# New instruction orders for two spectral convolutions and the attention front between them, and a strided read of kernel rows

## The chip, the cores and the metric

The kernel runs on one core of a Trainium2 chip. The metric is device time in microseconds (us) of one execution; lower is better. Five engines work in parallel and each takes its instructions in the order of the program: PE (matrix products into PSUM), VectorE (DVE), ScalarE (ACT), GpSimd (POOL) and SyncE (SP), which issues most DMA transfers.

## The reference, cut to what matters

Four layers follow each other on an activation `x` of 2048 rows and 512 columns in bf16, each with a layer normalisation ahead of it and a residual addition behind:

```python
x = x + _A_ref(_layernorm(x), A_wqkv, A_wo)      # sliding-window attention, 32 heads, 8 keys at distances 0, 2, .. 14
x = x + _B_ref(_layernorm(x), B_A_re, ..., B_Dskip)   # long convolution
x = x + _A_ref(_layernorm(x), A_wqkv, A_wo)
x = x + _B_ref(_layernorm(x), B_A_re, ..., B_Dskip)

def _B_ref(u, A_re, A_im, B_re, B_im, C_re, C_im, log_dt, Dskip):
    ...
    logdA, dB = dt * A, dt * Bc
    l = jnp.arange(L).astype(A_re.dtype)           # bf16: positions above 256 are rounded
    K = jnp.einsum("dn,dnl,dn->dl", Cc, jnp.exp(logdA[:, :, None] * l), dB).real
    ...                                             # y = causal convolution of u with K, by FFT of length 2 L
    return y + u * Dskip[None, None, :]
```

Both convolutions use the same filter `K` (one row of 2048 per column). Because the positions are in bf16, those from 256 on fall on even numbers, from 512 on multiples of four, and so on: `K` has only 641 different rows of 512 values.

## The kernel before

The program has stages, one after the other in each engine's stream:

1. *Filter and first front*: `k_gen` computes the 641 rows into a DRAM tensor `kd`, and beside it the first normalisation, queries and keys.
2. *First attention core*: `LayerA.core` with the order string `CORE0`. On the way `k_half_load` calls `k_load` twice (half the columns each): it fills `kr`, 128 partitions of 16 positions, from `kd`, with transfers issued by SyncE. `k_half_fix` (line 1501) adds `Dskip`; `k_part` (line 1505) reorders `kr` into `k_perm`.
3. *First convolution*: `FftB.run` with `ORDER0`.
4. *Rest of the first convolution and second front*: `FftB.run` with `ORDERF`.
5. *Second attention core* with `CORE1`; it begins with the last pieces of the front.
6. *Second convolution* with `ORDER1`, which ends in the stores to the output.

No scheduler chooses the order within a stage: each string is a list of tokens, worked off from left to right, and each token emits its instructions. What happens when is then set by the engines' in-order streams, by semaphores and by buffers. A convolution splits the columns into two groups g of 64 x 4, and has these tokens:

- `K`, `U` (`f1`, line 822): 16 matrix products transform a piece of the filter or of the input; 8 pieces for each group.
- `k`, `u` (`f2`, line 829): the second step, 16 small matrix products, 8 pieces for each group. `k` leaves the spectrum in a buffer; SyncE then issues two transfers that copy it with its halves swapped (line 854) and GpSimd issues one that keeps it in DRAM for the second convolution (line 855). `u` is always cast by ScalarE into one of three buffers `ub` (line 880).
- `m` (`u_mult`, line 868): VectorE multiplies `ub` by the spectrum and its swapped copy. In the second convolution the spectra come from DRAM through a ring (lines 858 and 860), ten pieces ahead.
- `y`, `Y` (`i1`, lines 894 and 898): back-transform, 8 pieces for each group; all eight `m` of the group must be done.
- `w`, `v`, `z` (lines 924 to 948): last step and residual addition into `x_sb`, for 8, 4 and 4 rows; the digits are group, half of its columns (not for `z`) and block of rows.

The letter behind a token names the engine that takes the result out of PSUM: `A` is ScalarE, `D` VectorE. With `D` a `w`, `v` or `z` piece is added by VectorE; with `A` PE adds the residual with further products and ScalarE casts. The PSUM tiles of a convolution (line 811 for the casts) come from two pools of two, taken round: a piece can be written once the piece four before it has been taken out.

Small letters at the start of `ORDER0` finish the first attention's last rows and their normalisation: `s`, `t` statistics, `g` aggregation, `r` reciprocal root on ScalarE, `a`, `e` the offsets, `c0` to `c7` the application (on GpSimd without a letter), `q` masks on GpSimd.

In `ORDERF` the convolution's last pieces stand between the front's: `h` and `H` statistics of half or whole rows (block b of four rows), `a` aggregation (line 1554), `p` reciprocal root (ScalarE, lines 155 and 156), `n` application (line 197; `G` shares it between GpSimd and VectorE), `T` transposes on PE (line 271), `E` their casts (line 273), `P` key projections (line 282, cast in line 285), `Q` query projection (line 223), `x` the shifted copy of keys (line 295), `S` the change of PSUM pools. `CORE1` begins with the pieces `P30`, `P31`, `x0`, `x2`, `P32`, `Q01`, `e0`, `Q02` and then the first product of queries and keys (line 342).

Of the kernel before, what the change touches and what calls it, by code (L numbers as in the profile page):

```python
# [21 lines left out]
S = 2048  # L22
# [27 lines left out]
lxzzppzEzektKxxkkkKEKteepkkkkKKkkkUUkUUUUUUEKKUoUUUUkkkoKkoUUpxxqqKQppxXXXpZZxxZ  # L50
"""
ORDER0 = """
KD a q KA c3 c1 t s KA KA KD KA g r KD e c2 KA KD KA c6 c0 c5A KD c7 kA kD c4D KA kA kD KA KD UA KD
UA UA UD KA UD UA UD UA kA kD kA kD u UD u UA UA m UD u u m m u u UA m m u u kD UA UA m m UA kD kA
kD m u u u kD kD kA kA m m m yA u u YA yD m yA m u u u yA YA yA m m m w000D yD yA YD yA YA yD yA
w010D
"""
ORDERF = """
yA h00 YA h01 v100A v110D h10 a0 z12A p0 z11A n0D h11 w001A w011A S a1 p1 T0 E01A z13A E00D n1G H2
P02 a2 P00 Q00 p2 T1 E10D E11D P01 P11 P12 n2D H3 a3 P13 T2 P10 E20D E21D P03 p3 P21 P22 n3D P23 T3  # L60
E30D E31A P20 x1
"""
ORDER1 = """
UA UD UA UD UA UA UD UA UD UD u u m m u u m m UA u UA UD m UA u u UD UA u m m u u m m u YD m u YA YA
m u yD m yA u u m m u w001A m m yA yA w000D YA yD yA YD w011D yA yD w010D yA yD yA v101A v103D v113A
v102D v112D v111D v110A v100A
"""

CORE0 = """
# [927 lines left out]
def bf16_round_np(x):  # L997
    x = np.ascontiguousarray(np.asarray(x, dtype=np.float32)); u = x.view(np.uint32)
    return ((u + 0x7FFF + ((u >> 16) & 1)) & 0xFFFF0000).view(np.float32)
# [409 lines left out]
def k_load(tc, nc, kr, kd, ds_):  # L1409
    l = np.arange(2048, dtype=np.float32)  # L1410
    m = bf16_round_np(l).astype(np.int64).reshape(128, 16) - 16 * np.arange(128)[:, None]
    nc.sync.dma_start(kr[0:16], kd[0:256, ds_].rearrange("(p a) d -> p a d", a=16))
    n = 1
    for o, (p0, p1, base) in enumerate(((16, 32, 256), (32, 64, 384), (64, 128, 512))):
        s = 2 << o
        blk = m[p0:p1]
        assert (blk == blk[0:1]).all() and (blk % s == 0).all()
        row = [int(v) for v in blk[0]]
        np_ = p1 - p0
        q = 16 // s  # L1420
        runs = []
        for v in range(0, 17, s):
            c = [a for a in range(16) if row[a] == v]
            assert c == list(range(c[0], c[-1] + 1))
            runs.append((v // s, c[0], len(c)))
        for (t, a0, cnt) in runs:
            rows = kd[base + t:base + t + (np_ - 1) * q + 1:q, ds_]
            nc.sync.dma_start(kr[p0:p1, a0:a0 + cnt, :],
                                                              rows.unsqueeze(1).to_broadcast([np_, cnt, D // 2]))
            n += 1  # L1430


@with_exitstack
def kernel(
# [58 lines left out]
    def k_half_load(h):  # L1493
        hs = slice(h * 256, (h + 1) * 256)
        kr = krp.tile([P, NA, D // 2], BF16, name=f"k_rl{h}")
        k_load(tc, nc, kr, kd, hs)
        krs[h] = kr
# [136 lines left out]
```

## Time and profile before

| | us |
|---|---|
| three runs | 396.95, 397.65, 400.25; median 397.65 |
| profiled execution: time | 397.01 |
| profiled execution: span on the core | 395.2 |
| busy: PE, DVE, ACT, POOL | 349.7, 377.4, 333.0, 43.2 |
| granted PE clock, mean | 0.996 |

The span is the time from the first to the last instruction on the core; the execution's own time has 1.8 us more around it. Stage bounds in the profiled execution: first cast of the first convolution at 183.78, last product of it at 230.40, first key projection of the second front at 247.47, first product of the second core at 263.18, first cast of the last convolution at 350.58. In a timeline row the columns are start, length, engine, line, operation, output and inputs, count, and in brackets the idle time before it with what ended it; `SPq` is SyncE's DMA queue. In a row of a waits view they are who waited for whom, the total, the count and the longest.

### The profile page before, as it was taken

Reading aid. Unit: us, or ns where it says so; the run is one execution under the profiler, and the core shown is the slowest. Engines: PE = TensorE matmul, PEld = TensorE weight load, DVE = VectorE, ACT = ScalarE, POOL = GpSimd, SP = SyncE. Lnnn points to the kernel's source line nnn. Section 1 sums busy time; section 2 is a strip of 40 time slices with the busy share of each in tenths; the row PEclk is TensorE's granted clock in tenths of the full one; section 3 lists DMA queues with packets and bytes.
Section 4 is the critical chain, followed back from the end, with each engine's and each line's share of the span. In section 5 each row is a group of like instructions: output and inputs, shape, how many; then the busy total and the mean of one; then the engine's idle time right before and its main releaser. Section 6 shows DMA issues by size and latency. Waiting matters only on the chain.

```text
span 395.2 us, 15021 instructions
## 1 busy us (share of the span) xinstructions
PE 349.7 (88%) x6598; PEld 240.5 (61%) x6598; DVE 377.4 (95%) x453; ACT 333.0 (84%) x594; POOL 43.2 (11%) x93
## 2 busy tenths in 40 slices
PE   3967568899999999999997889999999998887896
PEld 2225336585645677666886878543456676566885
DVE  6999999999999999999999999979999999989995
ACT  7999999999568789989999987675566899989974
POOL 9400100000370001002422200100000001000000
PEclk9999999899999999999999999999999999999999
DMA  7952811214125746494463844820153029504507
GB/s 211 398 162 35 86 53 25 71 29 87 57 50 133 211 149 195 111 347 172 174 237 131 309 124 109 307 67 0 40 162 95 3 78 347 157 14 152 174 3 215
DMA packets 63695, 54.18 MB, mean 137 GB/s; under 512 B 33033, under 2 KB 49966, under 8 KB 63374
## 3 DMA queue, kind: packets, MB, share of 16 engines
q1 hardware_dynamic: 61958, 48.70, 41.6%
q0 software_dynamic: 1664, 4.52, 3.1%
q8 instruction: 51, 0.84, 0.9%
q14 instruction: 14, 0.11, 0.1%
q10 hardware_dynamic: 8, 0.00, 0.0%
HBM read 30.15 MB, written 13.24 MB: 110 GB/s over the span
## 4 chain that ended last, share of the span: by engine, by line
DVE 35%; PE 32%; ACT 14%; issue 8%; DMA 7%; SPq 2%; POOL 1%; DVEq 0%; ACTq 0%; POOLq 0%
DVE pav L467 9%; PE pq L398 7%; ACT a1s L811 4%; PE pk L1323 4%; PE pp L1261 4%; PE pp L282 3%; PE pq L223 3%; DVE A_t L1157 3%; DVE prod L342 3%; DVE B_t L1157 3%; DVE t L868 2%; DMA w_sb<-w_dram 2%; PE L L350 2%; ACT ub L880 2%; DVE x_sb L946 2%
## 5 line engine op out<-in xcount | busy, mean ns | idle before, releaser
L467 DVE TENSOR_TENSOR pav<-attn,v_ext 128x4096 bf16<-128x4096 bf16 (+1 forms) x34 | 72.0, 2160 | 0.3
L342 DVE TENSOR_TENSOR prod<-qT,kT_ext 128x4096 bf16<-128x4096 bf16 x29 | 65.2, 2285 | 0.7 <-PE L L350 0.5
L1157 DVE TENSOR_TENSOR A_t<-A_t,pow_t 128x1024 bf16<-128x1024 bf16 (+4 forms) x46 | 38.0, 871 | 0.4
L492 PEld LDWEIGHTS <-pav 64*128 64x128 bf16 x1664 | 26.4, 95 | 14.1 <-DVE pav L467 6.7
L880 ACT CAST ub<-pb 128x1024 bf16<-128x1024 f32 x32 | 31.9, 1091 | 1.6 <-PE pb L829 1.0
L492 PE MATMUL po<-ident,pav 64*128 64x64 bf16 x1664 | 29.1, 191 | 4.6 <-ACT oT L484 1.8
L509 PE MATMUL pq<-wop,oT 128*128 128x512 bf16 x128 | 32.8, 380 | 0.3 <-ACT oT L494 0.2
L829 PE MATMUL pb<-a1s,w_sb 128*128 128x64 bf16 x768 | 27.6, 193 | 5.1 <-ACT ub L880 1.8
L398 PE MATMUL pq<-wv,xnT 128*128 128x512 bf16 x128 | 30.5, 380 | 0.0
L1261 PE MATMUL pp<-xnT,kT_ext 128*128 128x512 bf16 x96 | 24.7, 390 | 5.8 <-ACT xnT L1254 3.3
L829 PEld LDWEIGHTS <-w_sb 128*128 128x128 bf16 x768 | 24.9, 98 | 7.6 <-issue 5.9
L811 ACT CAST a1s<-pb 128x1024 bf16<-128x1024 f32 x29 | 28.1, 1064 | 1.1 <-PE pb L822 1.1
L400 ACT CAST v_ext<-pq 128x512 bf16<-128x512 f32 x32 | 18.6, 586 | 12.0 <-PE pq L398 11.9
L225 ACT CAST qT<-pq 128x512 bf16<-128x512 f32 x24 | 14.0, 584 | 12.8 <-PE pq L223 12.8
L1323 PEld LDWEIGHTS <-A_t 128*64 128x64 bf16 (+1 forms) x512 | 22.0, 105 | 4.5 <-issue 1.4
L1323 PE MATMUL pk<-B_t,A_t 128*64 128x84 bf16 (+1 forms) x512 | 23.9, 204 | 0.6 <-ACT kgs L1331 0.6
L811 DVE CAST a1s<-pb 128x1024 bf16<-128x1024 f32 x19 | 22.5, 1216 | 1.4 <-PE pb L822 1.3
L223 PE MATMUL pq<-xnT,kT_ext 128*128 128x512 bf16 x96 | 23.7, 380 | 0.0
L398 PEld LDWEIGHTS <-xnT 128*128 128x128 bf16 x128 | 11.7, 98 | 13.6 <-issue 1.3
L509 PEld LDWEIGHTS <-oT 128*128 128x128 bf16 x128 | 11.5, 98 | 12.7 <-ACT oT L494 2.2
L822 PE MATMUL pb<-F1c,xnT 128*64 128x128 bf16 x256 | 17.3, 219 | 1.6 <-ACT a1s L811 0.6
L1261 PEld LDWEIGHTS <-kT_ext 128*128 128x128 bf16 x96 | 8.7, 98 | 16.3 <-issue 8.4
(281 smaller groups left out, 911.9 us busy)
## 6 DMA issues: line engine op xcount, KB each, us to landing
w_sb<-w_dram SPq DMA_DIRECT2D x32, 256.0 KB, 5.7
w_dram<-xnT SPq DMA_DIRECT2D x1, 4096.0 KB
kf_ring<-kf_dram SPq DMA_DIRECT2D x13, 256.0 KB, 3.9
kf_ring<-kf_dram SPq DMA_DIRECT2D x26, 128.0 KB, 3.9
v_ext<-v_ext SPq DMA_DIRECT2D x4, 784.0 KB, 6.2
x_blk<-in_A_x_dram SPq DMA_DIRECT2D x4, 512.0 KB, 4.9
kT_ext<-in_A_wqkv_dram SPq DMA_DIRECT2D x4, 512.0 KB, 9.5
x_sb<-in_A_x_dram SPq DMA_DIRECT2D x4, 512.0 KB, 7.4
```

What stands on the lines that cost most here:

```text
L223: nc.tensor.matmul(pq[:], lhsT=self.wqk[:, dt, ft * P:(ft + 1) * P], rhs=self.xnT[:, dt, q * 512:(q + 1) * 512], start=(dt == 0), stop=(dt ...
L342: nc.vector.tensor_tensor(pr, self.qT[q][:, ft].unsqueeze(1).to_broadcast([P, W, 4, P]), kap, ALU.mult)
L398: nc.tensor.matmul(pp[:], lhsT=xnT[:, dt, a * P:(a + 1) * P], rhs=wv[:, dt, :], start=(dt == 0), stop=(dt == NDT - 1))
L467: nc.vector.tensor_tensor(pv[:, i], attn[:, n % 4].unsqueeze(2).to_broadcast([P, W, DH // parts, H]), vap, ALU.mult)
L492: nc.tensor.matmul(po[:, h, 0, i * nt + ft, :], lhsT=pvf[rows, i, w, ft * P:(ft + 1) * P], rhs=ident[rows, rows], start=(w == 0 and ft + i ...
L509: nc.tensor.matmul(pw[:], lhsT=oT[:, ftp, :], rhs=self.wo[:, ftp, :], start=False, stop=(ftp == NDT - 1), skip_group_check=ahead)
L811: (self.nc.scalar.copy if eng == "act" else self.nc.vector.tensor_copy)(dst, src)
L829: nc.tensor.matmul(p2[:, j, :], lhsT=self.w2[:, ec * EC + j, :], rhs=a1s[:, ec * EC + j, :], start=True, stop=True)
L880: nc.scalar.copy(ub[:], p2)
L1157: return lambda: nc.vector.tensor_tensor(*args)
L1261: nc.tensor.matmul(pps[kind, b, ft][:], lhsT=la.wqk[:, dt, c:c + P], rhs=la.xnT[:, dt, b * 512:(b + 1) * 512], start=(dt == 0), stop=(dt = ...
L1323: nc.tensor.matmul(o, lhsT=lhs, rhs=Bt[:, ri, c * CH + ql].rearrange("p b g -> p (b g)"), start=(not half and j % 4 == 0 and ri == 0), sto ...
```

## The change

Three order strings are replaced: `ORDER0`, `ORDERF` and `ORDER1`; `CORE0`, `CORE1` and `ORDERK` stay. The tokens are the same but for these: in `ORDER0` one `UD` becomes `UA`; in `ORDERF` `v100A` becomes `v100D` and `E20D` becomes `E20A`; in `ORDER1` one `yA` becomes `YA`, `v110A` becomes `v110D`, and `w011D` is split into `v012D` and `v013A`.

In `k_load` the second region (partitions 16 to 32, positions 256 to 511) has nine runs of equal positions, of 2, 1, 3, 1, 3, 1, 3, 1 and 1 places. It was read by nine transfers, one for each run, each row repeated as often as the run is long. Now four transfers read it: transfer c fills the places c, c + 4, c + 8 and c + 12 of every partition from every second row of `kd`. The bytes are the same. The two other regions take at most eight runs and keep their transfers. `k_load` runs twice, so ten transfers go. (The counter `n`, which nothing reads, goes too.)

```diff
 ORDER0 = """
-KD a q KA c3 c1 t s KA KA KD KA g r KD e c2 KA KD KA c6 c0 c5A KD c7 kA kD c4D KA kA kD KA KD UA KD
-UA UA UD KA UD UA UD UA kA kD kA kD u UD u UA UA m UD u u m m u u UA m m u u kD UA UA m m UA kD kA
-kD m u u u kD kD kA kA m m m yA u u YA yD m yA m u u u yA YA yA m m m w000D yD yA YD yA YA yD yA
-w010D
+q a KD KA t c2 KA KA s c1 g KD r c0 e KA KD c3 c5A KA KD KA KD c6 c4D KA c7 kA kD KA KD UA UA KD UA
+UD KA UD UA UD UA kA kD kA kD kA kD u u kD m UA UA UA UD UA m u kD u u m m kA UA kD kD u u UA UA m u
+m m kD u m kA u kA m u m u u m m yA YA yD m u u u m m m yA yA YA yD w000D yA yA YD yA YA yD yA w010D
 """
 ORDERF = """
-yA h00 YA h01 v100A v110D h10 a0 z12A p0 z11A n0D h11 w001A w011A S a1 p1 T0 E01A z13A E00D n1G H2
-P02 a2 P00 Q00 p2 T1 E10D E11D P01 P11 P12 n2D H3 a3 P13 T2 P10 E20D E21D P03 p3 P21 P22 n3D P23 T3
-E30D E31A P20 x1
+h00 yA YA v100D v110D w011A h10 a0 h01 p0 z11A n0D z12A h11 S w001A T0 a1 E01A p1 z13A E00D n1G P03
+H2 Q00 P00 T1 a2 p2 P01 P02 E10D E11D n2D H3 a3 P11 P12 T2 E20A P10 E21D p3 n3D P13 P21 x1 P20 T3
+E31A E30D P22 P23
 """
 ORDER1 = """
-UA UD UA UD UA UA UD UA UD UD u u m m u u m m UA u UA UD m UA u u UD UA u m m u u m m u YD m u YA YA
-m u yD m yA u u m m u w001A m m yA yA w000D YA yD yA YD w011D yA yD w010D yA yD yA v101A v103D v113A
-v102D v112D v111D v110A v100A
+UA UD UA UD UA UA UD UA UD UD u u m UA m u UA UD UA m u UD m u u UA m m u u u m u m m m u u YD YA YA
+m u yD yA m m yA u u w000D YA YA m m u m w001A v013A v012D w010D yD yA YD yA yD yA yD yA v102D v101A
+v111D v112D v110D v100A v103D v113A
 """
...
 def k_load(tc, nc, kr, kd, ds_):
...
-    n = 1
     for o, (p0, p1, base) in enumerate(((16, 32, 256), (32, 64, 384), (64, 128, 512))):
...
+        if len(runs) > 2 * s:
+            for c in range(2 * s):
+                t = row[c] // s
+                assert row[c::2 * s] == [row[c] + 2 * s * i for i in range(q // 2)]
+                rows = kd[base + t:base + t + np_ * q, ds_].rearrange("(p i) d -> p i d", i=q)[:, 0::2]
+                nc.sync.dma_start(kr[p0:p1, c::2 * s, :], rows)
+            continue
         for (t, a0, cnt) in runs:
             rows = kd[base + t:base + t + (np_ - 1) * q + 1:q, ds_]
             nc.sync.dma_start(kr[p0:p1, a0:a0 + cnt, :],
                                                               rows.unsqueeze(1).to_broadcast([np_, cnt, D // 2]))
-            n += 1
```

## The prediction

> **What bounds the kernel now.** I read the page first (whole span), then busy time in stretches cut where the orders meet, then VectorE's own waits, then the timelines of VectorE, ScalarE and SyncE inside each stretch. Lengths are us.
>
> ```profile
> span 395.2 us, 15021 instructions
> core 0: us, PE busy (x) PEld busy (x) DVE busy (x) ACT busy (x) POOL busy (x), PEclk, DMA share, GB/s
> 183.78:203.21 19.43, 18.25 (x556) 16.56 (x552) 19.15 (x25) 19.20 (x23) 8.91 (x14) 1.00 0.42 151
> 203.21:230.40 27.19, 22.14 (x685) 19.99 (x680) 26.25 (x24) 26.59 (x30) 4.63 (x9) 1.00 0.68 238
> 230.40:247.47 17.07, 16.23 (x346) 14.66 (x347) 15.53 (x40) 12.50 (x18) 0.64 (x1) 1.00 0.35 96
> 247.47:263.18 15.71, 15.71 (x108) 8.49 (x108) 13.67 (x36) 10.61 (x21) 1.04 (x2) 1.00 0.68 236
> 263.18:350.58 87.40, 82.99 (x1577) 48.93 (x1577) 85.47 (x72) 66.41 (x143) 1.03 (x1) 1.00 0.33 101
> 350.58:379.83 29.25, 24.93 (x727) 23.13 (x721) 28.63 (x25) 28.26 (x31) 0.00 (x0) 1.00 0.35 111
> 379.83:395.20 15.37, 11.37 (x352) 10.84 (x352) 10.67 (x12) 7.69 (x10) 0.00 (x0) 1.00 0.47 139
> ```
>
> The rows are: first convolution up to its last product (two rows), its tail with the start of the second front, the rest of that front, the second attention core, the last convolution, its tail. In the first two, VectorE (45.40 of 46.62) and ScalarE (45.79) are both full. In the third and fourth PE is the full one (31.94 of 32.78). In the core, and in the last convolution until its tail, VectorE is full. So a new order can only win the small gaps that are left; it can lose freely.
>
> ```profile
> DVE ln_nb L185 <- ACT ln_rstd L156: 1.4, 2, 0.8
> DVE t L868 <- DMA kn<-kn: 0.9, 1, 0.9
> DVE z L811 <- PE pb L898: 0.6, 1, 0.6
> DVE xnT L273 <- PE pt L271: 0.5, 1, 0.5
> DVE kT_ext L295 <- ACT kT_ext L285: 0.4, 1, 0.4
> ```
>
> These are VectorE's longest waits between 183 and 264 (total, times, longest). Only the second lies in the first convolution: a product waits for the transfer that swaps one kernel spectrum's halves.
>
> **The kernel rows.** Ten of SyncE's transfers go (five per half); the bytes stay, and so do the runs of 256 elements.
>
> ```profile
> 155.52 10.02 SPq L1428 DMA_DIRECT2D k_rl<-kd_dram  x17
> 165.65 10.99 SPq L599 DMA_DIRECT2D w_sb<-w_dram  x16
> 176.95 0.43 DVE L1505 COPY k_perm<-k_rl 128x1024 bf16<-128x1024 bf16 x1 [0.23 <-DMA w_sb<-w_dram]
> L829 PE MATMUL pb<-a1s,w_sb x512: 188/193/204, 189.4 to 224.7; 128*128 128x64 bf16 x171
> ```
>
> Seventeen issues took 10.02, 0.59 each, so five fewer free SyncE's queue about 2.9 earlier, in each half. The reader of the second half comes at 176.95, some 11 after the last of those issues; its 0.23 stands before an instruction with eight semaphores to look at. The cover is VectorE's attention products. Behind the reads in the queue stand the table stores and w_sb loads, whose first reader is the spectrum transform at 189.4. I take 0; ends -0.23 (the wait goes) and +0.6 (a strided transfer costs one more issue). Without the cover it would be worth 2.9.
>
> **First convolution, to its last product.** Each token of the order is a PE piece into one of four PSUM buffers, taken round, and a cast by VectorE or ScalarE; `m` is a VectorE product. `UD` fell from 5 to 4 and `UA` rose from 11 to 12; all else is permutation.
>
> ```profile
> 228.13 2.35 DVE L868 TENSOR_TENSOR t<-ub,kf_nat 128x2048 bf16<-128x2048 bf16 x2
> 193.27 6.53 ACT L811 CAST a1s<-pb 128x1024 bf16<-128x1024 f32 x7
> 225.78 1.22 DVE L868 TENSOR_TENSOR t<-ub,kn 128x2048 bf16<-128x2048 bf16 x1 [0.94 <-DMA kn<-kn]
> 227.09 1.01 ACT L880 CAST ub<-pb 128x1024 bf16<-128x1024 f32 x1 [0.59 <-DVE t L868]
> ```
>
> A VectorE piece takes 1.13 (2.35 - 1.22), a ScalarE cast about 0.92. VectorE ends the last product at 230.40 (the 228.13 row, 2 pieces, next piece at once). It loses one cast (1.13) and may lose the 0.94: floor 230.40 - 2.07 = 228.3. On ScalarE 46 casts stand up to the last `ub` in both orders (one `UA` more, one `yA` fewer ahead of it), so the last `ub` comes at 228.1 less its own 0.59 wait: 227.5, and the last product ends no earlier than 228.7. Laying the new sequence out by hand with these two durations and four buffers, I find VectorE waits of 0.55 at `UD11` (three `UA` in a row stand before it) and some 0.1 at each of four later products, and the last product at 229.0.
>
> The swaps and their queue then decide.
>
> ```profile
> 200.74 1.10 SPq L854 DMA_DIRECT2D kf_sb<-kf_sb  x2
> 206.70 2.07 SPq L854 DMA_DIRECT2D kf_nat<-kf_nat  x1
> 214.66 1.10 SPq L854 DMA_DIRECT2D w_sb<-w_sb  x2
> 224.01 2.81 SPq L854 DMA_DIRECT2D kf_nat<-kf_nat  x4
> kn<-kn SPq DMA_DIRECT2D x12, 128.0 KB, 4.7
> w_sb<-w_sb SPq DMA_DIRECT2D x4, 128.0 KB, 2.9
> ```
>
> Before, four spectra were swapped early, then four in a burst (8 transfers, 200.74 to 208.77: 1.00 each), one later, and seven in the last run (14 transfers, 214.66 to 226.82: 0.87 each, landing after 4.7). The new order moves two of the early ones (k2, k3) behind all U transforms, so seven (k2 to k8) come in one run, then four, then three: 28 transfers nearly without a gap, from 199.8 (one ScalarE cast before the old 200.74). By 0.87 the last is issued at 223.6 and lands at 228.3; the last product is due at 227.9. So it waits 0.4 and ends at 229.4, against 230.4. By 1.00 it lands at 231.9: that is the slow rival. I take 0.87, from the longer run of the two: **-1.0**; ends -1.7 and +2.6. Spreading the last three is what removes the old 0.94.
>
> **Its tail and the second front.**
>
> ```profile
> 235.93 1.22 DVE L946 TENSOR_TENSOR x_sb<-pb,x_sb 128x1024 bf16<-128x1024 f32 x1 [0.23 <-PE pb L944]
> 237.19 2.71 DVE L150 BATCH_NORM_STATS2 ln_bn<-x_sb 128x6 f32<-128x256 bf16 x8
> 239.82 0.67 DVE L946 TENSOR_TENSOR x_sb<-pb,x_sb 128x512 bf16<-128x512 f32 x1
> 246.43 0.99 ACT L273 COPY xnT<-pt 128x1024 bf16<-128x1024 bf16 x1
> 247.47 0.81 PE L282 MATMUL pp<-xnT,kT_ext 128*128 128x512 bf16 x3 [0.23 <-ACT xnT L273]
> 263.18 2.29 DVE L342 TENSOR_TENSOR prod<-qT,kT_ext 128x4096 bf16<-128x4096 bf16 x1
> ```
>
> One y more stands after the last `ub` on ScalarE (+0.92), which cancels part of the lead for the first piece of group 1; `w000D`, no longer behind the last product and a y, gives its buffer back sooner. I keep -0.8 at `w010D` (235.93). In the front, `v100` goes to VectorE (0.67) and `E20` to ScalarE (about 1.0), PE loses four small matmuls; `h01` moves behind `a0` and covers the wait for `p0` (0.5 of the 1.4), but half its old cover of `v100` goes (0.4). `E01A` moves ahead of `p1`, so PE no longer waits for it at 247.47; `E00D` ends 1.0 earlier. From there to the first product PE has the same 15.71 of work, and the order puts small waits in: `P21` on `E20A`, `E21D` (0.2), `x2` on `P23` (0.3). At 263.18 I keep **-0.6**. Bounds: -2.5 if PE's 0.84 of gaps goes too, +2.6 with the slow swaps. `p3` stands behind one more ScalarE piece; if `n3` slips, `T3` and all of the core slip with it.
>
> **The core** (263.18 to 350.58) keeps its order and its waits: 0.
>
> **Last convolution.**
>
> ```profile
> 386.73 1.21 DVE L811 CAST z<-pb 128x1024 bf16<-128x1024 f32 x1
> 388.18 0.69 DVE L946 TENSOR_TENSOR x_sb<-pb,x_sb 128x512 bf16<-128x512 f32 x1 [0.24 <-PE pb L944]
> 390.87 1.25 ACT L948 CAST x_sb<-pb 128x512 bf16<-128x512 f32 x2 [1.43 <-PE pb L944]
> 384.61 7.91 SPq L1597 DMA_DIRECT2D out_dram<-x_sb  x8
> ```
>
> VectorE loses `w011D` (1.13) and gains `v012D` and `v110D` (0.6 each): level. ScalarE changes `v110A` for `v013A`: level. The g0 additions move ahead of the g1 y pieces, and the last two additions go to two engines at once, not both to ScalarE (1.25): -0.6 there, less 0.2 for `m15`, whose `ub` now stands behind two whole `YA`. The eight small additions are still PE's, and the last store still takes 395.2 - 392.1 = 3.1. **-0.4**; ends -0.8 and +0.7 (the last three products, with `w000D` ahead of them, wait for two casts).
>
> **The sum.** 0 - 0.6 - 0.4 = -1.0. The profiled execution took 397.0 (span 395.2 and 1.8 around it), so 396.0. The median of the runs shown, 397.65, lies 0.65 above it: 396.6.
>
> **The rivals.**
> *Slow swaps (slower).* Place: SyncE's queue from 199.8, with the kf_dram stores on the same DMA engines. Price: at 1.00 per transfer the last product ends at 233.0, 2.6 late; all behind it is 2.6 late, less 0.4 at the end: 397.65 + 2.2 = 399.9. It decides from about 0.91 per transfer (28 x 0.04 = 1.1 eats the lead); the burst's six kf_nat transfers alone went at 1.14 (201.95 to 208.77), and at that the price would be 6.0. For it: 0.68 DMA share in 203.21:230.40 and the 2.07 issue in the burst; against: the old last run kept 0.87.
> The Trainium skill, "DMA: Bandwidth & Descriptors", section "Latency and other measured facts", has HBM answering in 0.2 us on average and 2 us at high load, the largest part of a transfer's fixed cost. The landing rows agree in kind (2.9 for w_sb, 4.7 for kn). If the longer run loads HBM more than the old one, as an estimate from that page up to 1.8 us would come on the last landing, and the forecast would become 398.4; this is why I give the slow side more than the fast.
> *No change.* PE is full in 230.40:263.18, and the extra y and the waits in the front take back the 1.0; the end gains nothing as PE's additions set it: 397.6. For it: 15.71 of 15.71; against: PE waits that the old order shows at 247.47.
> *All gaps go.* 228.7 for the last product, PE without its 0.84, -0.8 at the end: -1.7 - 0.8 - 0.8 = -3.3, 394.3. For it: VectorE idles 4.8 from 183.78 to 263.18; against: every wait removed there stands before a full PE.
> *It doesn't do what it says:* the four reads could leave the queue as slow as nine; it costs nothing (first part), so this is inside "no change".
>
> **How the numbers follow.** Forecast (about 395.5 to 397.2) 0.44, slow swaps 0.26, no change 0.20, all gaps 0.10. The predicted time is 396.6. The range takes in both rivals' ends: 394.0 to 400.6. One per cent, about what a measurement of this kernel can tell from no change, is 4.0. Beyond -4.0 goes only the last case, if PE's busy time, whose ends are modelled, hides more gaps than it shows: 0.09. Beyond +4.0 goes the slow rival from 1.08 per transfer on: 0.17. Within: 0.74.
>
> **What would show it.** Right: no product in the first convolution waits over 0.6 for a DMA; last product at 229 to 230; first product of the second core near 262.6; the last two additions start within 0.7 of each other on two engines; k_rl issues take 7 per half with no reader nearer. Wrong: `t<-ub` waits for swaps of 1 or more from the ninth on; PE gaps behind `T2` or `T3`; VectorE idle between 351 and 388; a wait at a k_perm copy.

## The result and the profile after

| | kernel before | changed kernel |
|---|---|---|
| median of 22 runs each, us | 397.78 (396.9 to 400.62) | 399.68 (398.59 to 401.5) |
| span of the profiled execution, us | 395.2 | 398.0 |
| mean granted TensorE clock | 0.996 | 0.987 |

The ratio of the times is 1.0037, 95% interval 1.0023 to 1.0051: 1.5 us slower by the ratio, 1.9 by the medians. The forecast was 1.0 faster. One execution of a kernel differs from the next by 1 us and more (see the ranges), so places are read from the profiles and sizes from many runs.

The reads of line 1428 of before now stand in lines 1429 (the four strided ones) and 1433, the `k_perm` copies of line 1505 in line 1509, and lines between 70 and 1411 have gone down by one. The view of busy time in stretches is cut at the same events as before: first cast of the first convolution, last product, `w010D`, first product of the second core, first cast of the last convolution, end. In both convolutions "first cast" is here VectorE's first (in the last one of before ScalarE's stands at 350.58, VectorE's at 351.03):

```profile
core 0: us, PE busy (x) PEld busy (x) DVE busy (x) ACT busy (x) POOL busy (x), PEclk, DMA share, GB/s
...
185.90:230.79 44.89, 38.04 (x1180) 35.00 (x1175) 44.22 (x46) 44.49 (x52) 10.54 (x19) 1.00 0.59 207
230.79:238.35 7.56, 6.34 (x224) 5.69 (x222) 4.80 (x5) 5.98 (x7) 0.00 (x0) 1.00 0.19 63
238.35:265.25 26.90, 26.14 (x272) 18.06 (x273) 24.38 (x70) 19.27 (x34) 1.68 (x2) 1.00 0.54 178
265.25:353.09 87.84, 81.98 (x1574) 49.40 (x1593) 85.46 (x72) 66.89 (x144) 1.03 (x1) 1.00 0.33 101
353.09:398.00 44.91, 35.83 (x1047) 33.68 (x1041) 39.55 (x37) 35.45 (x40) 0.00 (x0) 1.00 0.39 120
```

Against the same events before (183.78, 230.40, 235.93, 263.18, 351.03, 395.2), and with one more event ahead of them, VectorE's first `k_perm` copy of the second half (176.95 before, 177.40 after):

| stretch | before | after | difference |
|---|---|---|---|
| start to the first `k_perm` copy | 176.95 | 177.40 | +0.45 |
| head: to the first cast | 6.83 | 8.50 | +1.67 |
| products: to the end of the last one | 46.62 | 44.89 | -1.73 |
| tail: to `w010D` | 5.53 | 7.56 | +2.03 |
| front: to the first product of the second core | 27.25 | 26.90 | -0.35 |
| core: to the first cast of the last convolution | 87.85 | 87.84 | -0.01 |
| last: to the end | 44.17 | 44.91 | +0.74 |

The differences add up to the 2.8 between the spans. (The profile of before was among its shorter executions: 395.2 and 1.8 make 397.0, its median is 397.78.) So in the profiles the products won more than was forecast; the head, the tail and the last convolution lost it again.

*The head.* VectorE and then GpSimd in the changed kernel:

```profile
182.67 0.71 DVE L1509 COPY k_perm<-k_rl 128x1024 bf16<-128x1024 bf16 x1
183.31 0.86 DVE L196 TENSOR_SCALAR xnT<-x_sb,ln_rstd,ln_nb 128x512 bf16<-128x512 bf16 x1
184.09 0.41 DVE L1509 COPY k_perm<-k_rl 128x1024 bf16<-128x1024 bf16 x1
184.42 1.57 DVE L196 TENSOR_SCALAR xnT<-x_sb,ln_rstd,ln_nb 128x512 bf16<-128x512 bf16 x2
185.90 1.21 DVE L810 CAST a1s<-pb 128x1024 bf16<-128x1024 f32 x1
```

```profile
182.33 3.50 POOL L196 TENSOR_SCALAR xnT<-x_sb,ln_rstd,ln_nb 128x512 bf16<-128x512 bf16 x4 [25.55 <-PE po L491]
```

and in the kernel before:

```profile
182.15 0.41 DVE L1505 COPY k_perm<-k_rl 128x1024 bf16<-128x1024 bf16 x1
182.47 0.41 DVE L197 TENSOR_SCALAR xnT<-x_sb,ln_rstd,ln_nb 128x512 bf16<-128x512 bf16 x1
...
183.13 0.74 DVE L197 TENSOR_SCALAR xnT<-x_sb,ln_rstd,ln_nb 128x512 bf16<-128x512 bf16 x2
...
185.35 3.03 POOL L197 TENSOR_SCALAR xnT<-x_sb,ln_rstd,ln_nb 128x512 bf16<-128x512 bf16 x4 [28.51 <-DVE ln_nb L185]
```

The pieces are the same; of VectorE's five that fall beside GpSimd's four, four take 0.7 to 0.9 each, not 0.41 (the pair 1.57, not 0.74), and one, the copy at 184.09, still takes 0.41. Together that is 1.6 of the 1.67. The new order moves `a` ahead of the first `KD`, so VectorE makes the factors that GpSimd waits for before the cast and not behind it, and GpSimd starts 3 us earlier, into VectorE's copies.

*The tail.* VectorE from the last products on (bracket: idle before, and what ended it), then PE's wait of the y pieces for issue, summed from 183 to 398 (total, count, longest):

```profile
222.79 2.36 DVE L867 TENSOR_TENSOR t<-ub,kn 128x2048 bf16<-128x2048 bf16 x2 [0.27 <-ACT ub L879]
...
228.52 2.35 DVE L867 TENSOR_TENSOR t<-ub,kf_nat 128x2048 bf16<-128x2048 bf16 x2
230.79 1.22 DVE L810 CAST xnT<-pb 128x1024 bf16<-128x1024 f32 x1
...
233.66 1.22 DVE L810 CAST z<-pb 128x1024 bf16<-128x1024 f32 x1 [0.52 <-PE pb L893]
236.89 1.23 DVE L810 CAST z<-pb 128x1024 bf16<-128x1024 f32 x1 [2.01 <-PE pb L897]
```

```profile
PE pb L897 <- issue: 2.6, 3, 1.0
```

and in the kernel before VectorE's longest wait there, and PE's wait for issue of the y pieces:

```profile
234.47 1.22 DVE L811 CAST z<-pb 128x1024 bf16<-128x1024 f32 x1 [0.59 <-PE pb L898]
```

```profile
PE pb L898 <- issue: 0.2, 1, 0.2
```

The three waits of the changed kernel:

```profile
234.63 0.20 PE L897 MATMUL pb<-Wp,t 64*128 64x64 bf16 x2 [1.01 <-issue]
...
376.15 0.20 PE L897 MATMUL pb<-WpJ,t 64*128 64x64 bf16 x2 [0.74 <-issue]
...
389.19 0.20 PE L897 MATMUL pb<-WpJ,t 64*128 64x64 bf16 x2 [0.82 <-issue]
```

The 2.6 of "issue" are three waits in which nothing that the profile records was missing; before they were 0.2. All three stand in the y pieces (line 897). That leaves PE's own instructions. The page of the changed kernel has a DMA queue that carries instructions:

```profile
PE 346.4 (87%) x6531; PEld 241.2 (61%) x6578; DVE 378.3 (95%) x453; ACT 334.5 (84%) x595; POOL 43.7 (11%) x93
...
q8 instruction: 51, 0.84, 0.9%
```

51 packets of 0.84 MB are 16.5 KB each, and PE's 13,109 recorded instructions make 257 for each packet: one packet is a block of 256. Counted in the built program (weight loads and products; a product in f32 as the two loads and two products that the trace shows), the waits at the end of the first core (167.9, 173.3, 179.0) stand at instructions 3778, 4034 and 4290, and those at 234.6, 376.2 and 389.2 at 7106, 12226 and 12994: all six on one grid of 256, 194 beyond a multiple of it. This holds for every kernel below too. In the nineteen profiles PE has 45 waits of over 0.3 in which nothing recorded was missing; 44 of them stand 194 or 195 beyond a multiple of 256, and one (e8, 148.25) lies where records are missing and can't be placed. The transfers ahead of the wait at 234.6 (queue, packets, MB, share of the DMA engines), from 229.3 to 232.2 and then from 232.2 to 233.4:

```profile
q1 hardware_dynamic: 948, 0.94, 95.3%
```

```profile
q8 instruction: 1, 0.02, 5.9%
q1 hardware_dynamic: 18, 0.02, 4.5%
```

In the first stretch the weight reads for the second attention take 95.3% of the DMA engines, and no block comes. In the second the reads are done, and one block comes. PE goes on at 234.63, 1.2 after the block's end; at the waits at 376.2 and 389.2 it is 1.5 after it. The y pieces (32 matmuls and 32 weight loads in about 0.55) run through a block fast.

*The kernel rows and the swaps.* SyncE's queue:

```profile
155.46 2.52 SPq L1429 DMA_DIRECT2D k_rl<-kd_dram  x4
158.03 5.37 SPq L1433 DMA_DIRECT2D k_rl<-kd_dram  x8
163.50 10.32 SPq L598 DMA_DIRECT2D w_sb<-w_dram  x16
```

12 issues take 7.89, where about 7 was forecast (the four strided ones 2.52 of it, 0.63 each), and the w_sb reads start 2.15 earlier, not 2.9. No product waits for a swap: the row with 0.27 above is the longest wait of a product, and it is for a cast.

*The end.* VectorE, then ScalarE:

```profile
390.22 0.69 DVE L945 TENSOR_TENSOR x_sb<-pb,x_sb 128x512 bf16<-128x512 f32 x1 [0.49 <-PE pb L943]
391.37 2.70 DVE L945 TENSOR_TENSOR x_sb<-pb,x_sb 128x512 bf16<-128x512 f32 x4 [0.46 <-PE pb L943]
```

```profile
394.05 0.59 ACT L947 CAST x_sb<-pb 128x512 bf16<-128x512 f32 x1 [0.53 <-PE pb L943]
```

The last two additions are on two engines, as forecast, but at 393 to 394, behind y pieces that waited for the block at 389.19.

### The profile page after: what moved, and what is told of

The parts are those of the page before. It is cut to its first block, busy times and chain, and to the rows that moved or that the text cites. A ratio compares the mean times of both kernels' runs of the same rounds, so it can differ in the third digit from the quotient of the medians.

```text
span 398.0 us, 14927 instructions
## 1 busy us (share of the span) xinstructions
PE 346.4 (87%) x6531; PEld 241.2 (61%) x6578; DVE 378.3 (95%) x453; ACT 334.5 (84%) x595; POOL 43.7 (11%) x93
## 4 chain that ended last, share of the span: by engine, by line
PE 41%; ACT 25%; DVE 18%; issue 7%; DMA 5%; SPq 2%; POOL 1%; DVEq 0%; ACTq 0%; POOLq 0%
DVE pav L466 7%; PE pq L397 6%; PE pk L1322 4%; ACT a1s L810 4%; PE pq L222 4%; PE pp L1260 4%; PE pp L281 3%; DVE prod L341 3%; PE pb L828 3%; DMA w_sb<-w_dram 2%; PE pb L897 2%; ACT ub L879 2%; PE L L349 2%; PE pb L893 2%; ACT ws L1109 2%
## 5 line engine op out<-in xcount | busy, mean ns | idle before, releaser
L508 PE MATMUL pq<-wop,oT 128*128 128x512 bf16 x113 | 30.7, 380 | 2.7 <-issue 1.3
L810 ACT CAST a1s<-pb 128x1024 bf16<-128x1024 f32 x30 | 29.1, 1070 | 1.1 <-PE pb L821 1.1
L1260 PE MATMUL pp<-xnT,kT_ext 128*128 128x512 bf16 x88 | 23.6, 390 | 6.5 <-ACT xnT L1253 3.3
L810 DVE CAST a1s<-pb 128x1024 bf16<-128x1024 f32 x18 | 21.2, 1215 | 1.6 <-PE pb L821 1.5
L1124 PE MATMUL pt<-ws,ident 128*128 128x512 f32 x16 | 10.8, 760 | 9.2 <-ACT ws L1109 8.3
L515 ACT ACTIVATE x_sb<-pq 128x512 bf16<-128x512 f32 x24 | 14.2, 592 | 5.1 <-PE pq L508 4.9
```

What stands on the lines that cost most here:

```text
L508: nc.tensor.matmul(pw[:], lhsT=oT[:, ftp, :], rhs=self.wo[:, ftp, :], start=False, stop=(ftp == NDT - 1), skip_group_check=ahead)
L810: (self.nc.scalar.copy if eng == "act" else self.nc.vector.tensor_copy)(dst, src)
L1260: nc.tensor.matmul(pps[kind, b, ft][:], lhsT=la.wqk[:, dt, c:c + P], rhs=la.xnT[:, dt, b * 512:(b + 1) * 512], start=(dt == 0), stop=(dt = ...
```

## The experiments

All ratios are against the kernel before on the same chip, 12 runs of the kernel each (22 of the changed kernel; 11 of e17, where one execution of 1148.7 us is left out). The table has the stretches of one profiled execution of each, as above (us; "k" is the start of the first `k_perm` copy). "Shifted n" means that n small PE instructions were added early on, so that all later ones stand n places further on in PE's stream. Where two ratios are compared, the uncertainty is worked out from their two intervals as if they were independent.

| run | k | head | products | tail | front | last | ratio (95%) |
|---|---|---|---|---|---|---|---|
| before | 176.95 | 6.83 | 46.62 | 5.53 | 27.25 | 44.17 | 1 |
| after | 177.40 | 8.50 | 44.89 | 7.56 | 26.90 | 44.91 | 1.0037 (1.0023 to 1.0051) |
| e1 four reads alone | 177.50 | 7.34 | 48.19 | 6.93 | 27.26 | 44.35 | 1.0036 (1.0012 to 1.0060) |
| e2 after, KD first | 177.37 | 7.34 | 45.34 | 7.27 | 26.89 | 44.75 | 1.0029 (1.0008 to 1.0050) |
| e3 after, shifted 112 | 177.02 | 8.49 | 44.89 | 6.48 | 26.88 | 44.93 | 1.0035 (1.0012 to 1.0058) |
| e4 first order alone | 177.65 | 8.58 | 44.89 | 6.56 | 27.23 | 44.26 | 1.0015 (0.9999 to 1.0030) |
| e5 three orders, old reads | 176.91 | 8.51 | 44.89 | 7.25 | 26.90 | 44.39 | 1.0013 (0.9990 to 1.0037) |
| e6 after, last order of before | 177.22 | 8.51 | 44.96 | 6.42 | 26.90 | 44.34 | 1.0001 (0.9976 to 1.0027) |
| e7 before, shifted 288 | 177.23 | 7.96 | 47.25 | 5.53 | 27.26 | 44.21 | 1.0029 (1.0002 to 1.0055) |
| e8 KD first, front, old last, shifted 112 | 179.30 | 6.82 | 44.94 | 6.48 | 26.90 | 45.50 | 0.9986 (0.9960 to 1.0011) |
| e9 eight reads alone | 177.22 | 6.83 | 46.71 | 5.53 | 27.25 | 44.32 | 1.0010 (0.9988 to 1.0032) |
| e10 after, KD first, shifted 112 | 176.83 | 7.05 | 45.59 | 6.19 | 26.89 | 45.30 | 1.0019 (0.9996 to 1.0042) |
| e11 before, shifted 160 | 176.82 | 6.94 | 46.72 | 5.53 | 27.25 | 44.29 | 1.0010 (0.9992 to 1.0029) |
| e12 after, eight reads | 177.00 | 8.50 | 44.88 | 7.07 | 27.01 | 44.30 | 1.0023 (1.0004 to 1.0041) |
| e13 first order, KD first | 176.82 | 6.83 | 44.91 | 7.36 | 27.27 | 44.26 | 0.9986 (0.9966 to 1.0007) |
| e14 the same and second front | 176.98 | 6.83 | 45.29 | 7.30 | 26.91 | 44.24 | 0.9996 (0.9972 to 1.0020) |
| e15 the same, four reads | 177.26 | 7.06 | 45.30 | 7.27 | 27.01 | 44.34 | 0.9985 (0.9965 to 1.0006) |
| e16 the same, eight reads | 177.71 | 6.83 | 45.29 | 7.53 | 27.02 | 44.38 | 0.9960 (0.9937 to 0.9983) |
| e17 as e16, shifted 112 | 177.33 | 6.94 | 45.30 | 6.48 | 26.90 | 45.20 | 0.9982 (0.9956 to 1.0008) |

### The head of the first order (e2, e4, e13)

```diff
-q a KD KA t c2 KA KA s c1 ...        changed kernel
+KD a q KA t c2 KA KA s c1 ...        e2; e13: the same in the new first order, all else of before
```

e2. 

> The changed kernel, with the first cast KD put ahead of q and a in the first convolution's order, as it was before; nothing else. Theory (the a step ahead of the cast releases GpSimd's four normalisations about 3 us earlier, beside VectorE's k_perm copies and normalisations, which then take 0.7 to 0.8 each and not 0.41): those pieces fall back to 0.41, the first cast comes at 184.3 (185.90 in the changed kernel), time -1.5 us against the changed kernel. Rival (the delay there is TensorE's starvation alone): first cast stays at 185.5 or later, time 0 to -0.3.

e4, the new first order as written, all else of before. 

> The kernel before with only the new order of the first convolution. Theory: first cast +1.5 (185.3) by GpSimd beside VectorE, the products win 1.7 (last one ends at about 230.2), the wait for a late instruction block of about 1.0 in the tail comes back near 234, first product of the second core about 264.5 (263.18 before); time +1.2 us. Rival (the new order pays as predicted, the loss of the change lies in the kernel rows and in the last order): time -1.0.

e13. 

> The kernel before with only the new first order, and in it KD put back ahead of q and a. Theory (the early a step costs 1.2 at the head; the rest of the first order wins 0.7 from first cast to w010D): first k_perm copy to first cast 6.8 to 7.4, first cast to w010D 51.4 (52.15 before); time -0.7 us against the kernel before, 1.2 less than the new first order as it was written. Rival (the head is made up for later): level with the first order as written, +0.5.

VectorE of e2, and its GpSimd:

```profile
182.57 0.41 DVE L1509 COPY k_perm<-k_rl 128x1024 bf16<-128x1024 bf16 x1
182.89 0.41 DVE L196 TENSOR_SCALAR xnT<-x_sb,ln_rstd,ln_nb 128x512 bf16<-128x512 bf16 x1
...
183.55 0.75 DVE L196 TENSOR_SCALAR xnT<-x_sb,ln_rstd,ln_nb 128x512 bf16<-128x512 bf16 x2
184.71 1.23 DVE L810 CAST a1s<-pb 128x1024 bf16<-128x1024 f32 x1 [0.41 <-PE pb L821]
```

```profile
186.28 3.78 POOL L196 TENSOR_SCALAR xnT<-x_sb,ln_rstd,ln_nb 128x512 bf16<-128x512 bf16 x5 [29.70 <-DMA g_sb<-g_dram]
```

The pieces are back at 0.41 and GpSimd starts behind the cast: the theory holds in the trace. Over all profiles the head takes 8.49 to 8.58 with `a` first (six) and 6.82 to 7.96 with `KD` first (thirteen). The times follow less clearly. e2 is 0.3 us below the changed kernel (uncertainty 1.0), not the 1.5 that was expected; that is the time of its rival. The same edit is made twice more: e13 is 1.2 below e4 (1.0), and e10 is 0.6 below e3 (1.3). Weighted by their uncertainties the three pairs give 0.7 us, with an uncertainty of 0.6. So this cost is shown in the trace in every profile, and in the times at about half of what the profile has.

e4 came out at +0.6 where +1.2 was expected: its tail had no late block. e13's -0.6 was expected (-0.7), but not on the way it took: its late block was there (0.81 at 232.20), and from the first cast to `w010D` it took 52.27, not 51.4. Its agreement in the time is luck, as far as its profile tells.

### The late blocks (e3, e7, e11, e10, e17)

```diff
+SQ_PAD = {k: 7 for k in range(3, 11)}          e3, e8, e10, e17; 18 in e7, 10 in e11
...
             re = pst.tile([P, 4 * P], F32, name="pt")
+            for _ in range(SQ_PAD.get(k, 0)):
+                nc.tensor.matmul(re[:, 0:16], lhsT=ident[:], rhs=nident[:, 0:16], start=True, stop=True)
```

e3. 

> The changed kernel with 56 tiny TensorE matmuls (weight load and matmul, 112 instructions) added in TensorE's idle time in the squaring stages between 17 and 47 us, so that every later instruction stands 112 places further on in its instruction stream; they write columns that the next matmul overwrites. All orders are those of the changed kernel. Theory (TensorE's stream comes in blocks of 256 instructions, and it waits where it runs through a block in less than some 3.5 us or where the fetch meets a DMA burst): the issue waits of 1.01 at 234.6, 0.74 at 376.2 and 0.82 at 389.2 go, one of 0.8 or less comes at about 387, w010D comes 1.0 earlier; time -1.0 to -2.0 us against the changed kernel. Rival (these waits belong to the new order of the y pieces): all three stay at their places, time 0 to +0.3.

e3's VectorE:

```profile
235.42 1.22 DVE L810 CAST z<-pb 128x1024 bf16<-128x1024 f32 x1 [0.93 <-PE pb L897]
...
387.91 3.50 DVE L945 TENSOR_TENSOR x_sb<-pb,x_sb 128x512 bf16<-128x512 f32 x5
```

The wait ahead of the cast is 0.93, not 2.01, and the last additions run without one. No wait of a y piece for issue is left behind 183. So the waits belong to places in the instruction stream, not to the pieces: the theory holds there, the rival falls. The theory's 3.5 us is no threshold: the kernel before ran through the block that ends at 386.05 in 2.86 without a wait. What counts is when the block's packet has come: PE goes on 1.2 to 1.5 behind its end at each wait of the changed kernel, and in e4 and e6, where the block of the tail came 1.45 and 1.37 ahead of its use, PE did not wait: just in time. Of the ten profiles with the new first order and no shift, eight show the late block in the tail (7.07 to 7.56) and two do not (6.42 and 6.56); of the four with the shift, none (6.19 to 6.48). The time did not follow: -1.0 to -2.0 was expected, and 1.0035 is level with the changed kernel. The profile says where at least part went: the last cast ends at 391.97, 2.7 earlier than in the changed kernel, the span at 396.5, 1.5 earlier. The store tail took 4.5 instead of 3.4.

e7. 

> The kernel before with 144 TensorE matmuls and weight loads of 128 by 16 added (288 instructions, 18 pairs in each of the eight squaring stages between 16 and 47 us), which they overwrite afterwards: all orders are those of before, but TensorE's instruction stream is cut into blocks 32 places off (288 less 256). Theory: small, the blocks still end outside the runs of y pieces: issue waits after 200 of 0.5 or less in sum, time 0 to +0.5. Rival (the added matmuls themselves cost): the squaring stages end later than 47.6 and everything behind them by as much.

e11. 

> The kernel before with 160 TensorE instructions (80 tiny pairs) in the idle time of the squaring stages; nothing else. Theory: one block now ends inside the y pieces of the first convolution's tail, between 233 and 235; it is asked for during the burst of weight reads at 229 to 232, so TensorE shows an issue wait of 0.6 to 0.9 there, the second front starts as much later, and the time is +0.6 to +0.9 us against the kernel before. Rival (the waits belong to the new orders): no issue wait there, time 0.

e7 did what was expected after 200 (no wait for issue of a y piece; tail 5.53), but its time, +1.2, is outside the expected 0 to +0.5. Its products waited 1.37 for swaps, and its first cast waited 0.82 for PE. The reason for the second stands ahead of it, PE and VectorE of e7:

```profile
178.31 1.89 PE L482 MATMUL po<-ident,pav 128*128 128x128 bf16 x31 [1.51 <-issue]
```

```profile
185.19 1.23 DVE L811 CAST a1s<-pb 128x1024 bf16<-128x1024 f32 x1 [0.82 <-PE pb L822]
```

and PE of the kernel before at the same pieces, without a wait:

```profile
176.44 1.95 PE L482 MATMUL po<-ident,pav 128*128 128x128 bf16 x32
```

The shift put the end of a block (instruction 4546, again 194 beyond a multiple of 256) into these 32 products, and its packet came from 175.95 to 177.06 under the w_sb reads. PE stood 1.51 and then had work without a gap of more than 0.2 up to the first cast. This is the opposite proof: a wait put into the kernel before by a shift of the stream alone, though at the head and not in the tail. e11, which was made for the tail, is a miss: tail 5.53, no wait. Its block was expected behind the burst of weight reads and came in the middle of it, 1.95 ahead of its use. The price of a block in a burst is therefore not a fixed one.

e10, both repairs on the changed kernel. 

> The changed kernel with both repairs: KD put back ahead of q and a, and the 112 TensorE instructions in the squaring stages. Theory (the two losses are independent): k_perm copy to first cast 6.8 to 7.4 (8.50 in the changed kernel), last product to w010D 6.5 (7.56), no DVE wait for late y pieces in the last tail; time -1.5 to -2.2 us against the changed kernel, so level with the kernel before. Rival (each repair is taken back further on): -0.5 or less.

e17. 

> The fastest version so far (new first order with KD put back, new second front, last order of before, eight strided reads) with the 112 TensorE instructions in the squaring stages. Theory: the late block of 1.0 at 233 to 234 goes (no issue wait between 225 and 250), last product to w010D 6.5 (7.53 without them); time -0.8 us against that version, -2.4 against the kernel before. Rival (the block's wait is hidden or comes back elsewhere): level with it, -1.6 against the kernel before.

In e10 head and tail did what was expected (7.05 and 6.19) and the span is 395.7, 2.3 below the changed kernel's; in the times it is 0.0018 lower (0.7 us), half of what was expected and not separable. One y piece of its last convolution still waited 0.50 for issue (384.98), which was not expected. In e17 the tail fell from 7.53 to 6.48, and the last stretch grew from 44.38 to 45.20; the time is not lower than e16's. In all four kernels with the 112 instructions the end comes 4.1 to 4.5 after the last cast, in the others 3.1 to 3.4. What holds up the last stores there was not settled. So the three pairs with and without the shift (e3 and the changed kernel, e10 and e2, e17 and e16) differ in the times by -0.1, -0.4 and +0.9, each with an uncertainty of 1.1 to 1.4: the late blocks are shown in the traces, a price of theirs in the whole time is not.

### The kernel rows (e1, e9, e12, e15, e16)

```diff
+                h = np_ // 2                                                   e9, e12, e16
-                nc.sync.dma_start(kr[p0:p1, c::2 * s, :], rows)
+                nc.sync.dma_start(kr[p0:p0 + h, c::2 * s, :], rows[0:h])
+                nc.sync.dma_start(kr[p0 + h:p1, c::2 * s, :], rows[h:np_])
```

e1, the four reads with all else of before. 

> The kernel before, with only the four strided reads of the kernel rows taken from the change. Theory (TensorE's own instructions come by DMA in blocks of 16 KB, and a block that is asked for while the DMA engines are full comes late): the w_sb reads start about 2 us earlier, their full DMA share falls on the blocks fetched at 163 to 177, TensorE shows more waits put down to issue between 165 and 180 (1.5 or more in sum, 0.3 before), and the first cast of the first convolution moves from 183.8 by +0.3 to +0.5; time +0.4 us. Rival (freed queue time costs nothing, as predicted): no new issue waits, first cast at 183.8, time 0.

e9, the same in eight. 

> The kernel before with the strided reads of the kernel rows, each of the four cut into two halves by partitions, so that eight transfers (not four, and not nine) are issued; the strided pattern and the bytes stay. Theory (what the four reads alone cost, +1.4, comes from the w_sb reads and all that follows starting 2 us earlier in the queue): the w_sb reads start within 0.7 of the old 165.6, time 0 to +0.5 against the kernel before. Rival (the strided pattern itself costs): time +1.2 to +1.6, as with four.

e12. 

> The changed kernel with each of its four strided kernel-row reads cut into two halves by partitions (eight issues). Theory (the earlier queue costs): -0.5 to -1.0 us against the changed kernel, like the three new orders with the old reads. Rival (the strided pattern costs, or the reads cost nothing): 0 against the changed kernel.

e15 and e16, on the base of e14 (described below). 

> The same, with the kernel rows read by the four strided transfers. Theory (the four reads cost by the earlier queue): +1.0 to +1.4 against the run with the old reads. Rival (they cost nothing; the earlier difference was scatter): within 0.4 of it.

 

> The same, with each of the four strided transfers cut into two by partitions. Theory (the earlier queue costs, not the pattern): within 0.4 of the run with the old reads, whose queue it restores. Rival (the pattern costs): as slow as with four.

Alone the four reads came out 1.4 us slower with an interval that leaves out zero. Two more pairs compare four reads with nine: the changed kernel is 1.0 above e5 (uncertainty 1.1), and e15 is 0.4 below e14 (1.3). Weighted, the three give a cost of 0.8 us, with an uncertainty of 0.6. Eight reads against four are faster in all three pairs (e12 and the changed kernel 0.6, e9 and e1 1.0, e16 and e15 1.0), together 0.8 with an uncertainty of 0.6. Four and eight have the same strided pattern, so the pattern does not explain this.

The theory of the earlier queue fits part of it. PE's waits for issue between 165 and 180 add up to 0.3 and 1.0 with nine reads (before, e5), to 0.8 and 1.1 with eight (e9, e16) and to 1.7, 2.2 and 0.9 with four (e1, the changed kernel, e15). For e1 1.5 or more was expected, and its head took 0.51 longer, as expected too. But e9, whose time came out as expected, did not restore the queue: its w_sb reads start at 167.77, not within 0.7 of 165.65. And e15 came out within the bounds of its rival, which has no cost; e16, 1.4 below e14, fits neither of its theories. So a cost of the four reads of some 0.8 is likely and not shown, and its place is open.

e1's profiled execution was the slowest of its twelve (401.18), and has most of its loss in places that the old first order is known for, waits for swaps:

```profile
231.89 1.23 DVE L868 TENSOR_TENSOR t<-ub,kf_nat 128x2048 bf16<-128x2048 bf16 x1 [1.38 <-DMA kf_nat<-kf_nat]
```

With two more (0.49 and 0.37) they come to 2.24 in all, 0.94 before, and the tail took 6.93. The waits in the old order differ from profile to profile (products 46.62 to 48.19 in five profiles, 44.88 to 45.59 in fourteen with the new one). Whether e1's other runs had as many is not known.

### The other orders (e5, e6, e14, e8)

e5. 

> The kernel before with the three new orders; the kernel rows are read as before, by nine transfers. Theory (the kernel rows cost nothing beside the new first order, which no longer waits for the swaps; the loss is the head of the first order, its tail with a late instruction block, and the last order): time +1.5 to +1.9 us, like the change. Rival (the four reads carry the loss, as the run with them alone suggests: +1.4): time 0 to +0.4.

e6. 

> The changed kernel with the last convolution's order of before. Theory (the new order ends its arithmetic no earlier and bunches the last stores): from the first cast of the last convolution to the end of the span 44.3, against 44.91 in the changed kernel, no issue wait at 388 to 389; time -0.6 us against the changed kernel. Rival (the new last order pays 0.4, as predicted): 45.3, time +0.4.

e14. 

> The same, with the new second front too; kernel rows and last order of before, nothing added on TensorE. Theory: -0.35 more from w010D to the first product of the second core (26.9, 27.25 before), so -1.0 us against the kernel before if no late block falls in the tail, -0.2 if one does. Rival: 0.

e8. 

> A version that takes what paid: the new first order with KD put back ahead of q and a, the new second front, the last order and the kernel rows of before, and the 112 TensorE instructions in the squaring stages. Theory, by the lengths of the profiles so far: first order -0.7 from first cast to w010D, second front -0.35, head +0.4, no late block at 234: time -0.7 us against the kernel before. Rival (these lengths are scatter between executions): time 0 to +0.6.

e5 lies between its two theories (+0.5) and tells neither. e6, the changed kernel with the last order of before, is 0.0036 below the changed kernel (1.4 us, uncertainty 1.2): more than its stretch gives (44.34, not 44.91), and helped by a tail without a late block. The new front is shorter in every profile (26.88 to 27.02; 27.23 to 27.27 with the old one). e14 came out at -0.2, as expected with a late block, and it had one (0.75 at 232.68); its interval is too wide to tell the 0.35. e8 came out at -0.6 where -0.7 was expected, with an interval that takes in 1, but its profile has a last stretch 1.3 longer than before, which its theory did not have.

The only version whose interval lies below 1 is e16: new first order with `KD` put back, new second front, eight strided reads, last order of before, 0.9960. Its siblings e14 and e15 have 0.9996 and 0.9985, and its profile is no shorter than theirs; its profiled execution (398.35) was one of the slower of its twelve. A gain of 0.4 per cent is measured for it once and not explained, and one interval of eighteen can lie below 1 by chance.

## Why the prediction was wrong

- **The step that failed first: "all else is permutation".** The head of the first order was never costed. The new order has `a` ahead of the first cast, and I looked at PE, VectorE and ScalarE but not at whom `a` releases. GpSimd started 3 us earlier and slowed VectorE: +1.67 in the profile, 0.7 with an uncertainty of 0.6 in the times. It had its row in the trace of before (GpSimd's four pieces at 185.35, behind the cast).
- **First convolution, -1.0.** Right in direction, too small: -1.73 from the first cast, the end of the bound I gave (-1.7, the last product without any wait for a swap). No swap was waited for; the slow rival did not come. The new order also narrows this stretch (44.88 to 45.59 in fourteen profiles, 46.62 to 48.19 in five with the old one); the times do not get quieter by that alone (e4's twelve runs lie within 0.6 us, e14's within 4.6).
- **The tail, "I keep -0.8 at w010D".** I gave the tail +0.2 for one more y piece behind the last `ub`; 5.53 became 7.56. What counts for this stretch is that eleven y pieces stand behind the last product, seven before. Four pieces cost 0.95 (6.48 without a late block). Without a block the sum of products and tail is -0.8 after all (51.37 in e3, 51.44 in e4 and 51.38 in e6, 52.15 before): two terms that were each off by about 0.7 and cancel, which is luck. The rest, 1.08 in this profile, is the block, for which the prediction had no term; behind 150 us the trace of before shows such a wait with 0.34 at most.
- **Second front, -0.6.** Its own part was put at +0.2 (from -0.8 to -0.6). It is -0.35 here, and shorter than the old front by 0.2 to 0.4 in every profile.
- **Core 0.** Right (87.84).
- **Last convolution, -0.4.** The arithmetic does end earlier where no block is late (e3: 40.40 from first cast to last cast, 41.09 before), but in the changed kernel blocks are late at 376.15 and 389.19, and in e3 the stores take it back (4.5 from the last cast to the end). Measured +0.74 in the profile.
- **Kernel rows, 0.** The saving at issue was put too high (2.9; it is 2.1), and no reader waited longer, as forecast. But the prediction asked only who reads the rows, and not what the w_sb reads meet when they start 2.15 earlier. Three pairs of runs give a cost of 0.8, with an uncertainty of 0.6, and one of the three goes the other way; so 0 is doubtful, and what would take its place is not shown.
- **The rivals.** "Slow swaps" gave the right time, 399.9, for a wrong reason. "No change" named the right mechanism for the tail ("the extra y"), and not its size.
- **What stays open.** The profile lost 2.8 and the times 1.5. In the times three terms stand just clear of their uncertainties: the head (0.7, uncertainty 0.6), the kernel rows (0.8 and 0.6) and the last order (1.4 and 1.2, from e6 alone). Of these only the head was also found in the trace, with its cause, in every profile. The late blocks were found in the traces and do not show in the times.

## What to carry to other kernels

When an order is permuted, follow each moved piece to every engine that waits for it, GpSimd too: work that is released earlier can land beside work that it slows down. Count how much is moved behind the event that is won, for that is where the win is given back. And a stretch in which PE issues many small matmuls has a supply of its own: read the waits named "issue", count instructions, and look at what the DMA engines carry when the next block is due.

## What the runs showed of the hardware that was not expected

PE's instructions come by DMA in blocks of 256 (16.5 KB), and a block that comes late stops PE: 0.61 to 1.01 at five places of the changed kernel, 1.51 in e7. PE goes on 1.2 to 1.5 after the end of the block's packet. The Trainium skill, "Runtime: NRT & Kernel Launch", section "Instruction fetch mechanics", has blocks of this size, fetched over the sequencer's own DMA queue and mostly hidden. The size agrees, and so does "mostly": at the other ends of blocks in the changed kernel PE waits 0.3 or less for issue.

VectorE's copies and normalisations between SBUF tiles take 0.71 to 0.86, not 0.41, beside GpSimd's normalisations (four of five do), and those take 0.88 each (3.50 for four), not 0.76; casts from PSUM stay at 1.2. The Trainium skill, "SBUF — State Buffer", section "SBUF: two separate sides", has the two engines share one pair of ports as an exclusive lock, which some kinds of VectorE instruction and GpSimd's hold for their whole length. The direction agrees; that the ports are the reason, no run here shows.
